# Constant rows of the key and query stacks: two memsets in place of one, and eight source rows in place of four

## The chip, the cores and the metric

The kernel runs on one core of one Trainium2 chip. The metric is the time of one execution on the device in microseconds (us), as the median of several runs; lower is better.

## The reference

Two branches read the same 2048 tokens of 512 features and are mixed by a gate of each token:

```
x = A_x                                           # 1 x 2048 x 512
g = sigmoid((x * gate_w).sum(-1, keepdims=True))
# a: attention, 32 heads of 16, each query sees itself and the 255 tokens before it
q, k, v = split(x @ wqkv);  scores = q.k * 16**-0.5, masked to the band
a = softmax(scores) @ v @ wo
# b: channel MLP, 512 -> 1792 -> 512
b = gelu(layernorm(x) @ w1 + b1) @ w2 + b2
out = g * a + (1 - g) * b
```

## The kernel before, in words

Every matmul operand is split into a high part and a low part, and products are summed from three matmuls (high by high, low by high, high by low). TensorE is thus the busiest engine.

The program has three stages. The first (to about 169 us) makes q, k and v from x, 512 tokens at a time, and at the same time the statistics of the layer norm and the normalised input of the MLP. The second runs the attention of eight groups of four heads and fills TensorE's gaps with the MLP's first product, in an order written out as a string. The third is the MLP's second product and the output product of the attention. The change touches the first stage alone.

**The stacks.** `qk` is one SBUF tensor of 128 partitions with four planes of 2048 columns: planes 0 and 1 (`qs`) hold queries, planes 2 and 3 (`ks`) keys. A head's 16 features stand in 48 rows (high, high or low, low), and two heads stand above each other with four rows between them, which carry a correction by the row maximum: on the keys' side those four rows are minus one, on the queries' side they start as zero. The data goes through DRAM: `qk_out` (L316) writes every 512 tokens of q and k into the tensor `qkd[g]` (the profile calls it `qk` too), one for each of four head groups `g`, whose slots are `HR` = 52 rows of 2048 numbers; `load_stacks` (L347; its DMA is L351) reads 100 rows by four planes back from it into partitions 14 to 113 of `qk`. The four rows between two heads (rows 48 to 51 of every second slot) are put into DRAM by `gaps(g)` (L219; its DMA is L222), once for each group: one DMA of zeros for the queries' slots (t = 0) and one of minus ones for the keys' slots (t = 1), 4 blocks of 4 rows of 8 KB each. The source of both is `qk` itself, before it is filled, in partitions that `load_stacks` never writes.

**Where the constants come from.** On GpSimd (POOL), `masks_first` (L200) zeroes partitions 0 to 31 of the keys' planes, and `masks` (L204) zeroes those of the queries' planes (L206), sets partitions 96 to 127 of all four planes to minus one (L207) and builds the small masks `tri` and `wide`. Behind that on POOL stand memsets of `v` (L584) and a part of the splitting of x (`lo_part`, L134).

**What sets the order.** A table of steps, one for each unit of 12 or 24 matmuls: `masks_first` stands at step 2, `masks` at step 3, `gaps(g)` at steps 8, 16, 20 and 24, the first four `load_stacks` at steps 11, 19, 29 and 44, and the first score blocks `s_pair` (matmul L364, which read `qk`) at steps 16, 18, 20 and so on. Each engine works through its own instructions in this order. Nearly all DMAs are issued by SyncE (SP), a few (`put(act, 0, h)` in `qk_out`) by ScalarE (ACT). The completion of these DMAs is counted on eight semaphores in turn (DMAHW0 to DMAHW7), and a DMA that takes one of them waits for the DMA that had it before. So a later DMA can be held up by an earlier one with which it shares no data.

Of the kernel before, what the change touches and what calls it, by code (L numbers as in the profile page):

```python
# [19 lines left out]
S = 2048  # L20
# [11 lines left out]
HG = H // NG  # L32
VW = 17
VR = 560
HR = 52
# [27 lines left out]
def gated_mix_kernel(ctx, tc: tile.TileContext, xt, x2, wq0, wqk, wv, wo, xa, gw, w1, w2, b1, b2, out):  # L63
    nc = tc.nc
    dve, act, pool, pe, sp = nc.vector, nc.scalar, nc.gpsimd, nc.tensor, nc.sync
# [18 lines left out]
    def get(key, tag, bufs, shape, dt=F32):  # L84
        return left[key].tile(list(shape), dt, name=nm(tag), tag=tag, bufs=bufs)
# [38 lines left out]
    def small(tag, bufs, shape, dt=F32):  # L124
        return consts.tile(list(shape), dt, name=nm(tag), tag=tag, bufs=bufs)

    def view(t, *ap, off=0):
        return bass.AP(tensor=t.tensor, offset=t.offset + off, ap=[list(x) for x in ap])

    def f32(t):  # L130
        return t.bitcast(F32)
# [31 lines left out]
    qkd = [dram.tile([2, HG, HR, S], F32R, name=f"qk{g}") for g in range(NG)]  # L163
# [3 lines left out]
    qk = get("ring", "qk", 1, (128, 4, S), F32R)  # L167
    qs, ks = [qk[:, pr] for pr in range(2)], [qk[:, 2 + pr] for pr in range(2)]
# [35 lines left out]
    def masks():  # L204
        for t in qs:
            pool.memset(f32(t[:32]), 0.0)  # L206
        pool.memset(f32(qk[96:128]), -1.0)  # L207
        one = small("scr", 2, (128, 256), BF16)
        pool.memset(one, 1.0)
        pool.affine_select(out=one[:, :128], in_=one[:, :128], pattern=[[-1, 128]], base=0, channel_multiplier=1,  # L210
                           compare_op=ALU.is_ge, fill=0.0)
        for e in range(2):
            pool.tensor_copy(tri[:, e], one[:, :128])
        pool.memset(wide, 0.0)
        pool.memset(rt, 0.0)
        pool.affine_select(out=wide[:, 128:], in_=wide[:, 128:], pattern=[[-1, 128]], base=0, channel_multiplier=1,
                           compare_op=ALU.is_ge, fill=NEG)

    def gaps(g):  # L219
        for t in range(2):  # L220
            dst = view(qkd[g], [S, 4], [2 * HR * S, 4], [1, S], off=(t * HG * HR + 48) * S)
            sp.dma_start(f32(dst), f32(qk[124 * t:124 * t + 4]))  # L222

    wq, wvs, xh, xl = {}, [], [], []

# [357 lines left out]
    for i in range(4):  # L583
        at((3, 5, 6, 8)[i], lambda i=i: pool.memset(vs[:, 4 * i:4 * i + 4], 1.0))  # L584
    at(2, masks_first)
    at(3, masks)
    at(9, load_consts)
    for g in range(NG):
        at((8, 16, 20, 24)[g], lambda g=g: gaps(g))
# [199 lines left out]
    t = spare[0]  # L789
# [183 lines left out]
```

## Time and profile before

| | |
|---|---|
| median of 3 runs | 720.65 us (718.29 to 720.96) |
| the profiled execution's own time | 715.11 us |
| its span | 713.1 us, granted TensorE clock 0.99 in the mean |
| TensorE matmul (PE) busy | 688.7 us, 97% of the span |
| VectorE (DVE) / ACT / POOL busy | 479.6 / 384.3 / 270.5 us |
| moved by DMA | 138.42 MB, mean 194 GB/s |

A row of a timeline has the start, the duration, engine, line, operation, what is written and read, how many instructions are merged in it (x12), and in brackets how long the engine sat idle before it and what ended that. SPq is SP's sequencer; its rows are issues of DMAs, and their duration is the time that the issue took, not the transfer. A row of the windows has the stretch, its length, the busy time and instructions of the five engines, the granted TensorE clock (1.00 is full speed), the mean busy share of the 16 DMA engines and the GB/s that they moved.

### The profile page before, as it was taken

What the parts mean: (1) busy time and instruction counts of PE and PEld (TensorE: products, weight loads), DVE (VectorE), ACT (ScalarE), POOL (GpSimd) and SP (SyncE); (2) the same over time, 40 slices, a digit from 0 to 9 for tenths busy, and PEclk for the clock granted to TensorE, in tenths of its full rate; (3) what the DMA queues carried; (4) which work ended last, traced back from release to release, by engine and by line L of the source; (5) the groups of instructions that cost most, each with busy time, mean ns of one, the idle gap of its engine ahead of it and who ended that gap; (6) DMA issues with size and microseconds to landing.
All of it is one profiled execution on the core that took longest, in us unless ns stands there. A gap on an engine that the chain in (4) does not pass through costs nothing.

```text
span 713.1 us, 15508 instructions
## 1 busy us (share of the span) xinstructions
PE 688.7 (97%) x5674; PEld 537.8 (75%) x5674; DVE 479.6 (67%) x970; ACT 384.3 (54%) x637; POOL 270.5 (38%) x621
## 2 busy tenths in 40 slices
PE   9996897999999999999999999999999999999997
PEld 6675675787776877777787777877788888888886
DVE  6825555997777778777867788784675645646554
ACT  6315344344767777687676776767753323224131
POOL 6900104652666666576555664747500000000000
PEclk9998999999999999999999999999999999999999
DMA  9868767878766676757766756644686541750801
GB/s 327 295 197 245 202 162 225 258 226 260 219 217 189 175 228 211 232 154 212 226 209 186 224 165 187 184 148 145 230 289 225 182 154 40 213 178 9 268 8 60
DMA packets 88987, 138.42 MB, mean 194 GB/s; under 512 B 12048, under 2 KB 35984, under 8 KB 88784
## 3 DMA queue, kind: packets, MB, share of 16 engines
q1 hardware_dynamic: 80752, 129.24, 58.2%
q10 hardware_dynamic: 8160, 8.19, 4.0%
q8 instruction: 45, 0.74, 0.4%
q14 instruction: 30, 0.25, 0.1%
HBM read 82.06 MB, written 54.30 MB: 191 GB/s over the span
## 4 chain that ended last, share of the span: by engine, by line
PE 76%; DMA 13%; DVE 6%; ACT 2%; SPq 1%; issue 1%; ACTq 0%; POOL 0%; DVEq 0%
PE ps_a L882 21%; PE ps_b L652 20%; PE ps_b L442 12%; PE ps_b L419 7%; PE ps_b L364 6%; PE ps_o L851 6%; DMA t<-in_xa 4%; DMA qk<-qk 3%; DMA t<-in_x 2%; PE ps_d L309 2%; PE ps_d L341 2%; DMA t<-in_wqk 2%; DVE x L134 1%; DVE t L533 1%; DVE wv L236 1%
## 5 line engine op out<-in xcount | busy, mean ns | idle before, releaser
L652 PE MATMUL ps_b<-x,w 64*128 64x512 f32 x1344 | 207.3, 393 | 0.0
L882 PE MATMUL ps_a<-x,t 128*128 128x512 f32 x648 | 149.6, 389 | 0.0
L374 DVE TENSOR_REDUCE mx<-ps_b 128x2 f32<-128x512 f32 x208 | 144.1, 693 | 7.1
L882 PEld LDWEIGHTS ps_a<-x,t 128*128 128x128 f32 x648 | 121.6, 188 | 25.3
L652 PEld LDWEIGHTS ps_b<-x,w 64*128 64x128 f32 x1344 | 127.1, 186 | 10.7 <-ACT x L137 0.3
L373 DVE COPY_PREDICATED ps_b<-tri,ps_b 128x256 f32<-128x256 uint8 x208 | 88.3, 425 | 54.7 <-PE ps_b L364 42.1
L423 POOL TENSOR_SCALAR_AFFINE_SELECT pa<-pa 128x256 f32<-128x256 f32 x192 | 74.2, 414 | 56.3 <-ACT pa L421 55.3
L309 PE MATMUL ps_d<-x,w 128*128 128x512 f32 x360 | 89.6, 406 | 3.1 <-ACT v L137 3.1
L421 ACT ACTIVATE pa<-ps_b 128x768 f32<-128x768 f32 x96 | 76.6, 813 | 25.2 <-PE ps_b L419 14.5
L419 PE MATMUL ps_b<-qk 50*128 50x384 f32 (+5 forms) x512 | 88.0, 340 | 0.1
L309 PEld LDWEIGHTS ps_d<-x,w 128*128 128x128 f32 x360 | 70.5, 197 | 19.5 <-ACT v L137 3.6
L364 PE MATMUL ps_b<-qk 62*128 62x384 f32 (+3 forms) x472 | 83.1, 346 | 1.7 <-DMA qk<-qk 1.3
L421 ACT ACTIVATE pb<-ps_b 128x768 f32<-128x768 f32 (+2 forms) x96 | 66.2, 707 | 20.1 <-PE ps_b L419 10.5
L423 POOL TENSOR_SCALAR_AFFINE_SELECT pb<-pb 128x256 f32<-128x256 f32 x160 | 62.3, 415 | 37.8 <-ACT pb L421 37.2
L708 ACT ACTIVATE t<-t,b1s 128x512 f32<-128x512 f32 x56 | 38.6, 716 | 44.3 <-DMA t<-hp 43.8
L419 PEld LDWEIGHTS ps_b<-qk 50*128 50x128 f32 (+1 forms) x512 | 48.7, 184 | 16.7 <-issue 3.2
L423 POOL TENSOR_SCALAR_AFFINE_SELECT x<-x 128x256 f32<-128x256 f32 x128 | 49.3, 414 | 30.4 <-ACT x L421 29.9
L364 PEld LDWEIGHTS ps_b<-qk 62*128 62x128 f32 (+1 forms) x472 | 45.0, 184 | 18.6 <-issue 3.7
L421 ACT ACTIVATE x<-ps_b 128x768 f32<-128x768 f32 x64 | 50.7, 813 | 15.0 <-PE ps_b L419 10.9
L341 PE MATMUL ps_d<-wv,x 128*128 128x512 f32 x192 | 48.5, 399 | 1.1 <-DVE wv L236 0.8
L851 PE MATMUL ps_o<-w,t 128*128 128x512 f32 x192 | 46.1, 389 | 0.0
L341 PEld LDWEIGHTS ps_d<-wv,x 128*128 128x128 f32 x192 | 35.4, 188 | 11.9 <-DVE wv L236 2.0
(96 smaller groups left out, 772.3 us busy)
## 6 DMA issues: line engine op xcount, KB each, us to landing
qk<-qk SPq DMA_DIRECT2D x56, 400.0 KB
t<-hp SPq DMA_DIRECT2D x56, 256.0 KB
hp<-t SPq DMA_DIRECT2D x54, 256.0 KB
qk<-t SPq DMA_DIRECT2D x48, 256.0 KB
osc<-x SPq DMA_DIRECT2D x31, 256.0 KB
t<-in_w SPq DMA_DIRECT2D x28, 256.0 KB
w<-w SPq DMA_DIRECT2D x28, 256.0 KB
qk<-t ACTq DMA_DIRECT2D x24, 256.0 KB
```

The source lines that it names most:

```text
L309: pe.matmul(o, a[:, dt * 128:(dt + 1) * 128], b[:, dt * C:(dt + 1) * C], start=n == 0, stop=n == 11)
L341: pe.matmul(o, x[:, a:a + 128], wvs[dt][:, k], start=n == 0, stop=n == 11)
L364: pe.matmul(o[:, e, :n], qs[pr][r:k, qb * 128:qb * 128 + 128], ks[pr][r:k, t0:t0 + n], start=True, stop=True)
L373: dve.copy_predicated(o[:, :, :128], tri, o[:, :, 256:384])
L374: dve.tensor_reduce(m, o[:, :, :256], mybir.AxisListType.X, ALU.max)
L419: pe.matmul(o[:, e, :w], ks[pr][r:k, kb * 128:kb * 128 + 128], qs[pr][r:k, kb * 128:kb * 128 + w], start=True, stop=True)
L421: act.activation(pt[:, :, :w], o[:, :, :w], AF.Exp, scale=0.25)
L423: pool.affine_select(out=pt[:, :, a:a + 128], in_=pt[:, :, a:a + 128], pattern=[[0, 2], [sgn, 128]], base=b, channel_multiplier=-sgn, comp ...
L442: pe.matmul(a[32 * h:32 * h + 32, at:at + w], vs[:, kb, v:v + 32], pts[p, kb][:, h, fr:fr + w], start=n == 0, stop=n == len(parts) - 1, sk ...
L652: pe.matmul(o[:, e], w[kt // 4][r:r + 64, k, m:m + 128], y[r:r + 64, a:a + C], start=n == 0, stop=n == 23)
L851: pe.matmul(a, x[:, g], wos[g][:, k], start=n == 0, stop=n == 11)
L882: pe.matmul(accs[c][b], x[:, b * 128:(b + 1) * 128], w, start=f == 0 and n == 0, stop=f == FT - 1 and n == 2)
```

## The change

The memset of minus ones is made for the keys' two planes, one instruction each, and no longer for the queries' planes. The planes of the queries thus have no minus ones to copy from, so `gaps` takes all its rows from the keys' planes: eight partitions with both planes (16 KB in one piece each) in place of four partitions with four planes. Zeros come from partitions 0 to 7 (before: 0 to 3), minus ones from partitions 116 to 123 (before: 124 to 127). In DRAM the same rows are written; each partition now fills two neighbouring rows of one block, where before a partition filled one row in each of the four blocks.

```diff
     def masks():
         for t in qs:
             pool.memset(f32(t[:32]), 0.0)
-        pool.memset(f32(qk[96:128]), -1.0)
+        for k in ks:
+            pool.memset(f32(k[96:128]), -1.0)
         one = small("scr", 2, (128, 256), BF16)
...
     def gaps(g):
         for t in range(2):
-            dst = view(qkd[g], [S, 4], [2 * HR * S, 4], [1, S], off=(t * HG * HR + 48) * S)
-            sp.dma_start(f32(dst), f32(qk[124 * t:124 * t + 4]))
+            dst = view(qkd[g], [2 * HR * S, 4], [2 * S, 2], [1, 2 * S], off=(t * HG * HR + 48) * S)
+            sp.dma_start(f32(dst), f32(qk[116 * t:116 * t + 8, 2:].rearrange("k r s -> k (r s)")))
```

On POOL the rows from the memsets of the stacks on are, before (a name carries a running number; L207 is the memset of minus ones, 8192 numbers in each of 32 partitions):

```order
L206 MEMSET qk_75 32x2048 x2
L207 MEMSET qk_75 32x8192
L209 MEMSET scr_268 128x256
L210 ISA
L210 AFFINE_SELECT scr_268<-scr_268 128x128
```

and after:

```order
L206 MEMSET qk_75 32x2048 x2
L208 MEMSET qk_75 32x2048 x2
L210 MEMSET scr_269 128x256
L211 ISA
L211 AFFINE_SELECT scr_269<-scr_269 128x128
```

The one memset of 8192 numbers a partition is now two of 2048; nothing else on POOL has moved.

On SP, at the first call of `gaps`, before (`qk_65` is the DRAM tensor of group 0, `qk_75` the SBUF stacks; behind the two L222 stand a load of weights and stores of q and k):

```order
L322 DMA qk_65<-t_343 16x8x512 [waits DMAHW2_49,DVE_49]
L222 DMA qk_65<-qk_75 4x4x2048 [waits DMAHW3_49,Pool_49]
L222 DMA qk_65<-qk_75 4x4x2048 [waits DMAHW4_49,Pool_49]
L229 DMA t_394<-in_wqk 128x512 [waits DMAHW5_49]
L322 DMA qk_65<-t_409 16x8x512 [waits DMAHW6_49,Activation_49]
L322 DMA qk_65<-t_409 16x8x512 [waits DMAHW7_49]
```

and after:

```order
L323 DMA qk_65<-t_344 16x8x512 [waits DMAHW2_49,DVE_49]
L223 DMA qk_65<-qk_75 4x2x4096 [waits DMAHW3_49,Pool_49]
L223 DMA qk_65<-qk_75 4x2x4096 [waits DMAHW4_49,Pool_49]
L230 DMA t_395<-in_wqk 128x512 [waits DMAHW5_49]
L323 DMA qk_65<-t_410 16x8x512 [waits DMAHW6_49,Activation_49]
L323 DMA qk_65<-t_410 16x8x512 [waits DMAHW7_49]
```

The order and the waits are the same; the shape that the two DMAs write goes from 4x4x2048 to 4x2x4096. At the other three calls it is the same, and PE, DVE and ACT have the same rows with the same waits as before (line numbers behind the memset are higher by one).

## The prediction

> **What bounds the kernel.** I read the page's first two parts, then TensorE's waits in the first 170 us, where the changed lines lie, then PE's and SP's timelines there, and last windows over the stretches in which little moves. First the page: busy time, and tenths in 40 slices of 17.8 us.
>
> ```profile
> PE 688.7 (97%) x5674; PEld 537.8 (75%) x5674; DVE 479.6 (67%) x970; ACT 384.3 (54%) x637; POOL 270.5 (38%) x621
> PE   9996897999999999999999999999999999999997
> ```
>
> TensorE is the bound nearly everywhere; only slices 4, 5 and 7 (53 to 89 and 107 to 125 us) have holes. A change in the first stage is worth what it takes out of them. Who ends them (engine, tile, line; us, times, longest):
>
> ```profile
> PE ps_x L364 <- DMA qk<-qk: 10.3, 2, 7.1
> PE ps_d L309 <- ACT v L137: 3.1, 1, 3.1
> PE ps_x L364 <- DVE mx L374: 2.2, 2, 1.6
> ```
>
> and where they lie on PE:
>
> ```profile
> 49.90 2.88 PE L309 MATMUL ps_d<-x,w 128*128 128x512 f32 x12
> 59.87 0.69 PE L364 MATMUL ps_x<-qk 62*128 62x128 f32 x4 [7.09 <-DMA qk<-qk]
> 60.48 4.44 PE L309 MATMUL ps_d<-x,w 128*128 128x512 f32 x12
> 89.44 0.62 PE L364 MATMUL ps_x<-qk 62*128 62x384 f32 x4 [3.22 <-DMA qk<-qk]
> 113.24 7.36 PE L309 MATMUL ps_d<-x,w 128*128 128x512 f32 x24 [3.14 <-ACT v L137]
> 122.15 0.44 PE L364 MATMUL ps_x<-qk 62*128 62x384 f32 x2 [1.55 <-DVE mx L374]
> ```
>
> The two largest end when `load_stacks` lands. The same twelve matmuls take 2.88 us before the first hole and 4.44 us right behind it, 1.56 us more. So the holes hold 7.09 + 3.22 + 3.14 + 2.2 = 15.65 us, and 3 x 1.56 = 4.7 us if the second and third cost as much in slow matmuls: 20.3 us in all. This is the ceiling of a gain here.
>
> Why does `load_stacks` land late? SP's own rows (start, time of the issue), at the first, second and fourth `gaps` (L222):
>
> ```profile
> 32.50 1.04 SPq L222 DMA_DIRECT2D qk<-qk  x2
> 33.60 4.33 SPq L229 DMA_DIRECT2D t<-in_wqk  x1
> 38.02 3.71 SPq L322 DMA_DIRECT2D qk<-t  x1
> 45.29 0.48 SPq L229 DMA_DIRECT2D t<-in_wqk  x1
> 48.76 0.31 SPq L351 DMA_DIRECT2D qk<-qk  x1
> 65.82 0.84 SPq L222 DMA_DIRECT2D qk<-qk  x2
> 71.39 4.74 SPq L469 DMA_DIRECT2D t<-in_xa  x1
> 79.22 0.31 SPq L351 DMA_DIRECT2D qk<-qk  x1
> 97.50 0.61 SPq L222 DMA_DIRECT2D qk<-qk  x2
> 103.69 3.78 SPq L398 DMA_DIRECT2D qk<-md  x1
> ```
>
> The issue of a weight load takes 0.48 us at 45.29 us and 4.33 us right behind `gaps`; behind three of the four calls SP is stuck for 3.7 to 4.7 us at a time. Windows in those stretches (the last two figures are the share of the 16 DMA engines and GB/s), with one of undisturbed loads ahead:
>
> ```profile
> 10.00:20.00 10.00, 10.00 (x46) 8.28 (x45) 10.00 (x13) 6.07 (x12) 9.48 (x4) 1.00 1.05 404
> 36.00:38.00 2.00, 2.00 (x11) 1.65 (x10) 0.69 (x1) 0.60 (x1) 0.47 (x1) 1.00 0.24 25
> 70.00:72.00 2.00, 2.00 (x10) 1.66 (x9) 1.65 (x11) 1.73 (x5) 0.00 (x0) 1.00 0.31 32
> 106.00:108.00 2.00, 2.00 (x11) 1.27 (x10) 0.00 (x0) 0.00 (x0) 0.00 (x0) 1.00 0.17 18
> ```
>
> At full load the 16 engines move 404 GB/s, 25 each. At 36 us, 0.24 x 16 = 4 engines are busy and move 25 GB/s together: four engines at the rate of one. A `gaps` DMA has four partitions as source and four outer rows as destination. I read this as four engines that each take one partition, through one path into SBUF that carries 25 GB/s. Every other transfer has a share on those four engines and queues behind. So the constant rows are the choke of this stage, and not the memset.
>
> **The change part by part.** Sizes of the DMAs:
>
> ```profile
> qk<-qk SPq DMA_DIRECT2D x8, 128.0 KB
> ```
>
> *The DMAs of `gaps`.* A call moves 2 x 128 KB = 262 KB (decimal); at 25 GB/s that is 10.5 us, of which the stretch from the issue at 32.50 us to the return of normal issues at about 44.8 us is made. After, the bytes, the number of DMAs and the four outer destination rows are the same, but each DMA reads eight partitions, two for each engine. The trace has no DMA of eight rows, so its rate is bounded: at least 25 GB/s (all eight rows on one path: no gain), at most 100 GB/s (four engines at 25 each: 2.6 us a call). I take 50 GB/s. 404 GB/s over 128 rows is 16 paths of 25 GB/s, 8 rows each on the average, and four neighbouring rows were seen to share one; so eight neighbours need not fit on one path, and two paths is the nearest case. Then a call takes 5.2 us, 5.2 us less.
>
> Here a rule bears on the case. The Trainium skill (SBUF — State Buffer, Door 1: The DMA port swizzle) says that four neighbouring partitions share a port, and partitions 32 higher come back to it. By it 0 to 3 and 4 to 7 are on two ports, as are 116 to 119 and 120 to 123; with its ~27 GB/s a port, a call would take an estimated 4.9 us, and the sum below would differ by 0.3 us a call. The row at 36 us agrees for four partitions; no run here shows eight yet. The same skill (DMA: Bandwidth & Descriptors, Why a DMA increments its semaphore by 16 and not by 1) has a DMA use the largest number of engines up to 16 that divides the outer dims of both sides: 4 with 4 before, 4 with 8 after, so it speaks against any relief by more engines. The share of 0.24 agrees with four.
>
> *First hole.* `load_stacks` is issued at 48.76 us behind the stuck issues and lands at 59.87. If all moves up by 5.2 us, 1.9 us of the 7.09 stay. Is the matmuls' slow stretch gone too? Windows (granted clock is the third figure from the right):
>
> ```profile
> 59.90:64.80 4.90, 4.90 (x17) 3.92 (x18) 3.04 (x7) 3.94 (x10) 0.00 (x0) 0.63 0.92 320
> 118.50:124.00 5.50, 3.33 (x16) 2.18 (x15) 5.36 (x13) 2.33 (x6) 3.11 (x10) 1.00 0.78 227
> ```
>
> Behind the 7.09 us hole the clock is 0.63; over the two short waits on DVE (2.2 us together) it stays 1.00. With 1.9 us left I count the 1.56 us as saved. Term: 5.2 + 1.56 = 6.8 us.
>
> *Second hole.* The second pair's issue at 65.82 us is tied to PE's progress (it stands behind stores of its results), so it moves with PE, and the pair is again 5.2 us shorter; `load_stacks` at 79.22 us stands behind it. 5.2 is over 3.22, so the hole closes, with its slow matmuls: 4.8 us.
>
> *Third hole.* PE waits for ACT, and ACT sat idle until just before, released by one of its own issues of a store:
>
> ```profile
> 111.13 0.63 ACT L472 ACTIVATE waste<-t 128x512 f32<-128x512 f32 x1 [9.07 <-DMA qk<-t]
> ```
>
> This is the fourth pair's stretch (97.50 to about 110 us). Closed in full it is worth 3.14 + 1.56 = 4.7 us. But ACT also waits for loads of `in_xa` that lie in the same queues, so I take half, 2.3 us. The short waits on DVE I leave at nothing: DVE is busy 5.36 of 5.5 us there (the window above).
>
> *The memset.* POOL and DVE:
>
> ```profile
> 12.38 3.56 POOL L206 MEMSET qk<- 32x2048 f32 x2
> 16.00 6.95 POOL L207 MEMSET qk<- 32x8192 f32 x1
> 25.32 1.97 POOL L584 MEMSET v<- 128x2240 f32 x1
> 28.41 4.24 POOL L134 TENSOR_TENSOR x<-v,x 128x512 fp32r<-128x512 f32 x3 [1.12 <-ACT x L137]
> 16.89 7.72 DVE L236 CAST wv<-t 128x512 fp32r<-128x512 f32 x4
> 45.15 0.43 DVE L195 CAST w<-t 128x512 fp32r<-128x512 f32 x1 [7.33 <-DMA t<-in_wqk]
> 23.29 7.73 PE L341 MATMUL ps_d<-wv,x 128*128 128x512 f32 x24 [0.76 <-DVE wv L236]
> ```
>
> Two memsets of 2048 take 3.56 us where one of 8192 takes 6.95: POOL gains 3.4 us. What stands behind is done 3.4 us earlier up to 28.41 us, where POOL waits for ACT anyway. `gaps` is first issued at 32.50 us, 9.5 us after the memset's end: no gain there. One thing could be: four casts on DVE take 1.93 us each while POOL writes, where the same cast takes 0.43 later, and PE waits on them. But POOL's next memset of `v` moves up to 21.9 us and covers the fourth cast again, and what PE saves before 52 us it waits longer in the first hole. I count 0; the bounds are 0 and 0.76 us. The cover is the first hole; if the DMAs shrink so far that it closes, up to 0.76 us comes back.
>
> **Sum.** 6.8 + 4.8 + 2.3 = 13.9 us. The profiled execution took 715.11 us (span 713.1) and would take 701.2; it lies 5.5 us below the median of the three runs, 720.65, on which it gives 706.8. I say 707.
>
> **The rivals.** *One path in part.* If the 16 paths are blocks of eight neighbours, partitions 0 to 7 lie on one path and only 116 to 123 straddle two: a call goes from 10.5 to 7.9 us. The 404 GB/s row allows it as well. Then the first hole loses 2.6 us and keeps its slow clock, the second closes to 0.6 us and loses 2.6 + 1.56, the third half of 2.6: 8.1 us in the best case, about 5 if the holes follow by half: 713 to 716.
>
> *The choke is not at the rows read.* Four engines writing into one DRAM tensor could share the limit on that side, or the transfer is late for another reason; then eight rows read at 25 GB/s as four did, and only POOL's 3.4 us go, off the path: 720 to 721. For it speaks that no row tells source from destination; against it, that stores of results to DRAM do not show such windows.
>
> *Slower.* The destination of an engine changes too: before, the four engines wrote four neighbouring rows of one block, now each writes its own block, 104 rows of 8 KB away from the next. If the limit is at the DRAM side and blocks at that distance collide, a call gets longer. The slowest row above has 18 GB/s; at that, a call takes 14.6 us, 4.1 more. Passed on through three holes it is +12 us: 733. It decides from the point where the rate with only these transfers under way falls below 25 GB/s. Nothing in the trace speaks for it beyond that row, which is the tail of a call with fewer engines at work (share 0.17).
>
> **How the numbers follow.** A difference under 0.5% (3.6 us) is about what a measurement of this kernel cannot tell from none. Two paths for each DMA, 10 to 18 us gained: 0.62. Half the effect, 4 to 10 us: 0.18. No change: 0.14. Slower: 0.06. So faster 0.80, same 0.14, slower 0.06. The range goes from 701 (all holes of 20.3 us closed) to 718 (below it 0.62 + 0.18 and a little of "no change"; slower left out); the likeliest case's own is 702 to 711.
>
> **What would show it.** In the profile of the changed kernel: the windows with only `gaps` under way show 50 GB/s at a share near 0.25 and are half as long; the issue behind `gaps(0)` takes 1 to 2 us in place of 4.33; PE's hole before the first L364 is 1 to 3 us and the twelve matmuls behind it take 2.88 us; the hole at 89 us is gone. POOL's two memsets take 3.56 us and PE's wait on the casts stays near 0.76. I am wrong if the GB/s in those windows stay at 25, or if they double and another transfer (`in_xa`, `in_x`) keeps PE's holes as long as they are.

## The result and the profile after

The changed kernel takes 698.75 us (median of 4 runs, 697.51 to 699.18), the kernel before 719.71 us beside it (4 runs, 718.29 to 720.96): ratio 0.9707, 95% interval 0.9681 to 0.9732. That is 21 us faster where 13.9 were predicted, and below the stated range. A later measurement on another chip gave 699.48 us, ratio 0.9727 (0.9708 to 0.9746), 19.6 us by the ratio. The profiled execution took 697.51 us with a span of 695.5 us, 17.6 us shorter than before's 713.1.

Busy time and the tenths of PE in 40 slices, of the page of the changed kernel:

```profile
PE 684.8 (98%) x5674; PEld 537.5 (77%) x5674; DVE 475.4 (68%) x970; ACT 384.6 (55%) x637; POOL 268.2 (39%) x622
PE   9989999999999999999999999999999999999997
```

The three dents of before are one shallow one. Who ended PE's waits in the first 170 us, in the changed kernel (line numbers are one higher than before):

```profile
PE ps_x L365 <- DMA qk<-qk: 2.7, 1, 2.7
PE ps_x L365 <- DVE mx L375: 1.0, 2, 0.6
```

The waits for `load_stacks` fell from 10.3 to 2.7 us, the wait for ACT is gone. On PE's timeline:

```profile
22.78 5.60 PE L342 MATMUL ps_d<-wv,x 128*128 128x512 f32 x24
47.26 2.88 PE L310 MATMUL ps_d<-x,w 128*128 128x512 f32 x12
52.83 0.69 PE L365 MATMUL ps_x<-qk 62*128 62x128 f32 x4 [2.69 <-DMA qk<-qk]
53.45 5.49 PE L310 MATMUL ps_d<-x,w 128*128 128x512 f32 x12
80.92 5.76 PE L310 MATMUL ps_d<-x,w 128*128 128x512 f32 x24
98.97 5.60 PE L310 MATMUL ps_d<-x,w 128*128 128x512 f32 x24
```

Two things here were not forecast. The 24 matmuls on `wv` (first row) take 5.60 us without a wait, where they took 7.73 behind a wait of 0.76: PE reaches the first hole 2.64 us earlier (50.14 for 52.78). And behind a hole of only 2.69 us the twelve matmuls take 5.49 us, more than the 4.44 of before (granted clock 0.50 from 53.40 to 58.70 us). The second hole and its slow matmuls are gone as forecast; the third, of which half was forecast, is gone whole. The 24 matmuls behind them take 5.76 and 5.60 us, before 7.35 (the row below) and 7.36:

```profile
89.98 7.35 PE L309 MATMUL ps_d<-x,w 128*128 128x512 f32 x24
```

SP's issues at the first call of `gaps` (now L223) in the changed kernel:

```profile
29.37 1.43 SPq L223 DMA_DIRECT2D qk<-qk  x2
30.86 1.26 SPq L230 DMA_DIRECT2D t<-in_wqk  x1
42.84 0.32 SPq L352 DMA_DIRECT2D qk<-qk  x1
```

The load behind it is issued in 1.26 us (before 4.33), and `load_stacks` at 42.84 us (before 48.76). But the call itself is also 3.1 us earlier, which the prediction had ruled out. (The predicted sign of 50 GB/s at a share near 0.25 cannot be read off the windows of the changed kernel, since other transfers are under way too: from 63.90 to 64.90 us the share is 0.50, with 104 GB/s. The packets further below show the rate.) The source of the earlier call is on VectorE; the casts of `wv` before and after (minimum, median, maximum of the four in ns):

```profile
L236 DVE CAST wv<-t x4: 500/554/6342, 16.9 to 24.1; 128x512 fp32r<-128x512 f32 x4
```

```profile
L237 DVE CAST wv<-t x4: 503/894/2111, 17.4 to 21.1; 128x512 fp32r<-128x512 f32 x4
```

The mean of 1.93 us that the prediction used was no mean of four alike: one cast was held for 6.34 us, to the end of the long memset (22.95 us), the other three took about half a microsecond.

### The profile page after: what moved, and what is told of

Read it like the earlier page. It is cut to its first block, busy times and chain, and to the rows that moved or that the text cites. A ratio compares the mean times of both kernels' runs of the same rounds, so it can differ in the third digit from the quotient of the medians.

```text
span 695.5 us, 15509 instructions
## 1 busy us (share of the span) xinstructions
PE 684.8 (98%) x5674; PEld 537.5 (77%) x5674; DVE 475.4 (68%) x970; ACT 384.6 (55%) x637; POOL 268.2 (39%) x622
## 4 chain that ended last, share of the span: by engine, by line
PE 87%; DMA 8%; DVE 2%; ACT 1%; issue 0%; SPq 0%; ACTq 0%; POOL 0%; DVEq 0%
PE ps_a L883 22%; PE ps_b L653 21%; PE ps_b L443 12%; PE ps_d L310 8%; PE ps_b L420 7%; PE ps_b L365 6%; PE ps_o L852 6%; PE ps_d L342 4%; DMA qk<-qk 3%; DMA t<-in_x 1%; DMA gws<-in_gw 1%; DMA wv<-in_wq 1%; DVE t L477 1%; DMA stat<-ms 0%; DVE mx L375 0%; ACT x L422 0%
## 5 line engine op out<-in xcount | busy, mean ns | idle before, releaser
L420 PE MATMUL ps_b<-qk 64*128 64x384 f32 (+5 forms) x512 | 88.6, 340 | 0.1
L310 PE MATMUL ps_d<-x,w 128*128 128x512 f32 x360 | 87.4, 399 | 0.0
L365 PE MATMUL ps_b<-qk 62*128 62x384 f32 (+2 forms) x472 | 83.5, 346 | 1.0 <-DMA qk<-qk 0.8
L310 PEld LDWEIGHTS ps_d<-x,w 128*128 128x128 f32 x360 | 68.8, 192 | 15.4 <-issue 0.5
L342 PE MATMUL ps_d<-wv,x 128*128 128x512 f32 x192 | 47.0, 395 | 0.0
L443 PE MATMUL ps_b<-pa,v 128*32 128x128 f32 (+2 forms) x704 | 42.9, 345 | 0.7 <-POOL pb L424 0.4
```

Of the source, the lines that this page charges most:

```text
L310: pe.matmul(o, a[:, dt * 128:(dt + 1) * 128], b[:, dt * C:(dt + 1) * C], start=n == 0, stop=n == 11)
L342: pe.matmul(o, x[:, a:a + 128], wvs[dt][:, k], start=n == 0, stop=n == 11)
L365: pe.matmul(o[:, e, :n], qs[pr][r:k, qb * 128:qb * 128 + 128], ks[pr][r:k, t0:t0 + n], start=True, stop=True)
L420: pe.matmul(o[:, e, :w], ks[pr][r:k, kb * 128:kb * 128 + 128], qs[pr][r:k, kb * 128:kb * 128 + w], start=True, stop=True)
L443: pe.matmul(a[32 * h:32 * h + 32, at:at + w], vs[:, kb, v:v + 32], pts[p, kb][:, h, fr:fr + w], start=n == 0, stop=n == len(parts) - 1, sk ...
```

## The experiments

Each kernel was measured beside runs of the kernel before on the same chip, in three sets of runs on three chips. Before's medians in them were 718.20, 718.38 and 718.63 us; ratios are to these, and gains in us are worked out from the ratios unless medians are named.

**The memset alone.** Four neighbouring source partitions, in the changed kernel's order of the destination.

```diff
-        pool.memset(f32(qk[96:128]), -1.0)
+        for k in ks:
+            pool.memset(f32(k[96:128]), -1.0)
...
-            dst = view(qkd[g], [S, 4], [2 * HR * S, 4], [1, S], off=(t * HG * HR + 48) * S)
-            sp.dma_start(f32(dst), f32(qk[124 * t:124 * t + 4]))
+            dst = view(qkd[g], [2 * HR * S, 4], [2 * S, 2], [1, 2 * S], off=(t * HG * HR + 48) * S)
+            src = f32(qk[124 * t:124 * t + 4, 2:].rearrange("k r s -> k (r s)"))
+            sp.dma_start(f32(dst), src.unsqueeze(1).broadcast_to([4, 2, 2 * S]))
```

> The memset's part alone, with the destination order of the changed kernel: minus ones only in the keys' planes, and each of the four engines writes its own block in pieces of 16 KB, but the source is four neighbouring partitions (0 to 3, 124 to 127), each read twice. Theory A (four neighbouring partitions share one path of 25 GB/s; the memset's worth is a separate 2.6 us, since VectorE's first cast is blocked for as long as the memset runs, 6.34 us before): 2 to 4 us faster than before, 716 to 718; the window with only these transfers under way stays at about 25 GB/s with a share of 0.25, and PE's first hole stays near 7 us but begins 2.6 us earlier. Rival B (the memset is hidden by the first hole, as predicted): within 1 us of before. Rival C (the limit is on the DRAM side, and the new order of the blocks or the pieces of 16 KB relieve it): 18 us or more faster, the window at 50 GB/s.

Measured: 716.31 us, ratio 0.9971 (0.9953 to 0.9989). A window of this kernel with almost only these transfers under way, and PE's first hole:

```profile
33.00:34.50 1.50, 1.50 (x9) 1.23 (x8) 0.32 (x1) 0.60 (x1) 0.00 (x0) 1.00 0.33 33
```

```profile
57.56 0.69 PE L366 MATMUL ps_x<-qk 62*128 62x128 f32 x4 [7.73 <-DMA qk<-qk]
```

0.33 x 16 = 5.3 busy engines move 33 GB/s, 6.3 each, as before (25 by 3.8 engines, 6.5 each). So neither the new order in DRAM nor pieces of 16 KB relieve the choke, and rival C falls. The kernel gains 2.1 us (0.8 to 3.4). The hole stays but begins 2.95 us earlier, at 49.83 us (57.56 less 7.73), and does not grow by as much (7.73 us for 7.09), because `gaps` is issued earlier too (its row stands in the next section). So B falls as well, though the interval of the time alone would not quite exclude it. This run has the new order of the destination as well; no run has the shorter memset with the old order.

**The eight rows alone.** `gaps` as in the change, the memset as before.

> The eight source rows alone; the memset still covers all four planes (6.95 us). Theory A: 17 to 18.5 us faster than before, 701 to 703, thus 2 to 4 us slower than the changed kernel; the first cast on VectorE takes 6.3 us again, the window shows 50 GB/s. Rival B (memset hidden): 698 to 699, as the changed kernel.

Measured: 702.10 us, ratio 0.9784 (0.9758 to 0.9810), 15.5 us by the ratio. The rows carry most of the gain. Its casts are held for 5.74 us again.

**Four rows, moved by two partitions.**

```diff
-            sp.dma_start(f32(dst), f32(qk[124 * t:124 * t + 4]))
+            sp.dma_start(f32(dst), f32(qk[2 + 120 * t:6 + 120 * t]))
```

> The kernel before with the four source partitions moved by two: 2 to 5 for zeros, 122 to 125 for minus ones; memset, shape and destination as before. Theory A (paths are groups of four partitions starting at multiples of four): two partitions on each of two paths, so the transfers take half as long, and the kernel is 16 to 18.5 us faster than before, 701 to 704. Rival D (a path is a block of eight neighbours, or what counts is the number of source rows): no change, 719 to 721, window at 25 GB/s. Rival C (DRAM side): no change.

Measured: 703.49 us, ratio 0.9802 (0.9772 to 0.9831). Nothing but the partitions' numbers differs from before, and 14.2 us go. A window in the first call:

```profile
35.50:36.50 1.00, 1.00 (x6) 0.84 (x5) 0.35 (x1) 0.00 (x0) 1.00 (x1) 1.00 0.29 66
```

0.29 x 16 = 4.6 engines move 66 GB/s, 14 each, twice the rate of before. It is not the number of rows but the border that the range straddles: 2 to 5 and 122 to 125 lie on two paths each, 0 to 3 and 124 to 127 on one each. The prediction's rival of blocks of eight neighbours falls with it (2 to 5 are in one such block). The port map of the Trainium skill (SBUF — State Buffer, Door 1: The DMA port swizzle) has its border there; here the runs agree.

**Four rows, four partitions apart.** The changed kernel with another source:

```diff
-            sp.dma_start(f32(dst), f32(qk[116 * t:116 * t + 8, 2:].rearrange("k r s -> k (r s)")))
+            src = f32(qk[115 * t:115 * t + 13:4, 2:].rearrange("k r s -> k (r s)"))
+            sp.dma_start(f32(dst), src.unsqueeze(1).broadcast_to([4, 2, 2 * S]))
```

> The changed kernel with four source partitions four apart (0, 4, 8, 12 and 115, 119, 123, 127), each read twice, so that by theory A each of the four engines has a path to itself: a call of gaps takes 2.6 us (100 GB/s at a share of 0.25), the first hole of 2.7 us and the slow matmuls behind it (5.49 us for twelve in place of 2.88) go, 3 to 5.5 us faster than the changed kernel, 693 to 696. Rival E (with 50 GB/s the constant rows no longer bound anything, the loads behind them do): within 1.5 us of the changed kernel, 697 to 700.

Measured: 695.13 us, ratio 0.9680 (0.9657 to 0.9704), 3.6 to 4.4 us under the changed kernel's two medians. A window in the second call, and the place of the first hole on PE:

```profile
56.50:57.50 1.00, 1.00 (x6) 0.82 (x5) 0.91 (x3) 0.77 (x3) 0.00 (x0) 1.00 0.35 131
```

```profile
46.86 2.88 PE L311 MATMUL ps_d<-x,w 128*128 128x512 f32 x12
49.67 0.44 PE L366 MATMUL ps_x<-qk 62*128 62x128 f32 x4
50.04 2.99 PE L311 MATMUL ps_d<-x,w 128*128 128x512 f32 x12
```

5.6 engines move 131 GB/s, 23 each, near the 25 of undisturbed loads. The first hole is closed, and the twelve matmuls behind it run at full speed. 6.5, 14 and 23 GB/s for an engine with four, two and one of them on a path: the rate is divided among those that share it.

These windows hold some other traffic too, and their rates are estimates. The traces settle it, for they hold every DMA packet with its start, duration and size, and the packets of `gaps` differ by their size from those beside them on the queue: 8 KB, or 16 KB where both planes go out in one piece, against 2 KB. The first call, from its first packet to the end of its last:

| kernel | source partitions | first call |
|---|---|---|
| before | 0 to 3, 124 to 127 | 34.72 to 44.16 us, 9.4 us |
| memset alone | the same | 31.78 to 41.63 us, 9.9 us |
| eight rows alone | 0 to 7, 116 to 123 | 34.90 to 41.18 us, 6.3 us |
| changed kernel | the same | 31.33 to 37.17 us, 5.8 us |
| moved by two | 2 to 5, 122 to 125 | 34.98 to 40.82 us, 5.8 us |
| four apart | 0, 4, 8, 12 and 115, 119, 123, 127 | 30.46 to 33.80 us, 3.3 us |

In before the commonest time of an 8 KB packet is 1.25 us (9 of 32, 6.5 GB/s), and the shortest 0.31 us. With the rows moved by two 13 of 32 take 0.31 us and the next commonest time is 0.63 us (4). With spread rows 15 of 16 packets of 16 KB take 0.61 us (26.8 GB/s). So a packet takes about four, two or one times the shortest, as four, two or one engines share a path.

**One call at a time.** Memset as before; eight rows in the first call only, in the second only, in the third and fourth only.

```diff
+            if g == 0:    # or g == 1, or g > 1: the changed source and destination
+                ...
+            else:         # those of before
```

> The memset as before; only the first call of gaps takes its rows from eight partitions, the other three from four. The prediction's term for the first hole: 6.8 us faster than before. From the profile of the eight rows alone (first hole 3.03 us in place of 7.09, the twelve matmuls behind it still slow): 4 to 5 us faster, 713 to 714.5.

> As the run on the first call, but only the second call takes eight rows. The prediction's term for the second hole: 4.8 us faster than before, 713.4. If the first call's delay is what makes the second hole: under 2 us faster.

> As the run on the first call, but only the third and the fourth call take eight rows. The prediction's term for the third hole, counted at half: 2.3 us faster than before, 716. If the wait on ScalarE ends with the fourth call's transfers alone, the hole closes whole, with its slow matmuls and the waits on VectorE behind it: 4.5 to 6.5 us faster, 712 to 714.

Measured: first call 714.31 us, ratio 0.9942 (0.9917 to 0.9966), 4.2 us; second 714.64 us, 0.9941 (0.9919 to 0.9962), 4.2 us; third and fourth 712.15 us, 0.9907 (0.9874 to 0.9940), 6.7 us. The sum of 15.1 us is that of the eight rows alone (15.5): the calls add up. The holes do not divide as cleanly: with only the last two calls changed the third hole is gone and the wait for ACT with it, but the second shrinks too, from 3.22 to 1.59 us without slow matmuls, and a wait of 2.35 us on VectorE follows at 118.20 us. With only the first call changed, PE shows

```profile
54.73 0.44 PE L368 MATMUL ps_x<-qk 62*128 62x128 f32 x4 [1.82 <-DMA qk<-qk]
55.10 4.60 PE L313 MATMUL ps_d<-x,w 128*128 128x512 f32 x12
110.03 7.35 PE L313 MATMUL ps_d<-x,w 128*128 128x512 f32 x24 [4.15 <-ACT v L137]
```

A hole of 1.82 us, nearly the 1.9 that the prediction left, still costs slow matmuls; and the third hole stands as long as the last calls are slow.

**The memset in pieces.** Eight rows, and the memset over all four planes in 16 instructions of 512.

```diff
-        pool.memset(f32(qk[96:128]), -1.0)
+        for n in range(16):
+            pool.memset(f32(qk[96:128, n // 4, n % 4 * C:n % 4 * C + C]), -1.0)
```

> Eight rows as in the changed kernel; the memset of all four planes is as large as before (8192 numbers a partition) but cut into 16 instructions of 512. If a cast on VectorE is kept out for the whole of the POOL instruction that runs (one block of 6.3 us behind one long memset): the four casts take 2 to 4.5 us together though POOL writes as long as before, and the kernel gains 1.5 to 3 us on the run with eight rows alone, 699 to 701. If POOL's writing slows the casts in proportion (1.9 us each, as the mean of the row suggests): the casts take 7 us and the time stays at 701 to 703.

Measured: 703.07 us, ratio 0.9772 (0.9735 to 0.9808), not told from the eight rows alone. POOL and the casts:

```profile
16.05 7.47 POOL L208 MEMSET qk<- 32x512 f32 x16
```

```profile
L237 DVE CAST wv<-t x4: 500/554/6845, 17.0 to 24.7; 128x512 fp32r<-128x512 f32 x4
```

Both theories missed. The casts are not slowed in proportion (three take half a microsecond), but the first is not let in between 16 instructions back to back either: it waits 6.85 us, to the end of the last (23.52 us). In this run what counts is when POOL's run of writes ends.

**The memset shorter.** Spread rows; minus ones in one plane only.

```diff
-        for k in ks:
-            pool.memset(f32(k[96:128]), -1.0)
+        pool.memset(f32(ks[0][96:128]), -1.0)
...
+            dst = view(qkd[g], [2 * HR * S, 4], [S, 4], [1, S], off=(t * HG * HR + 48) * S)
+            src = f32(ks[0][115 * t:115 * t + 13:4])
+            sp.dma_start(f32(dst), src.unsqueeze(1).broadcast_to([4, 4, S]))
```

> The spread rows (0, 4, 8, 12 and 115, 119, 123, 127), with minus ones in one plane of the keys alone, which each of the four source partitions reads four times: POOL's memset takes 1.8 us in place of 3.6. If the length of POOL's writing still counts once the constant rows are quick: the casts take 2.5 us in place of 4.2 and the kernel gains another 1 to 2 us on the run with spread rows, 693 to 694. If PE has no hole left in which it could show: 694 to 696.

Measured: 693.07 us, ratio 0.9653 (0.9630 to 0.9677), the fastest kernel of this study, some 6 us under the changed one. Its casts:

```profile
L237 DVE CAST wv<-t x4: 503/556/1206, 16.9 to 19.0; 128x512 fp32r<-128x512 f32 x4
```

The four take 2.59 us, as the first theory had it. But that the 2.1 us to the spread rows come from this is not shown. They are from two sets of runs, and the intervals of the ratios overlap. And in the profiles PE is no earlier: its first twelve matmuls behind the first `s_pair` begin at 50.19 us, with spread rows at 50.04. The two part at 100 us, where the kernel with spread rows waits on VectorE for 1.36 and 0.61 us and its next twelve matmuls take 4.61 us, this one for 0.58 and 0.62 us and 3.02.

**The changed kernel again, and with the full memset in four instructions** (`for k in ks + qs`).

> The changed kernel itself, beside the others of this call on the same chip: 697.5 to 700; it says how much the next kernel's larger memset costs, and the spread rows gain, without a change of chip.

> The changed kernel with the memset of minus ones over all four planes again, but as four instructions of 2048 in place of one of 8192: only POOL's 3.5 us of extra writing tell it from the changed kernel. If the memset is worth what its run alone gained (2 us): 1.5 to 3 us slower than the changed kernel in this call. If with quick rows it is worth more (SP reaches the first call of gaps later by the whole delay of the casts): 3 to 5 us slower. If hidden: under 1 us.

Measured: 699.48 us (0.9727, 0.9708 to 0.9746) and 700.95 us (0.9755, 0.9734 to 0.9777): 1.5 us between the medians, and the intervals overlap. The three kernels with eight rows and the full memset, in one instruction, in sixteen and in four, gain 15.5, 16.4 and 17.6 us by their ratios; the changed kernel gains 21.1 and 19.6. So with quick rows the shorter memset is worth 2.0 to 5.6 us, and against the memset in one instruction the intervals do not overlap (0.9758 to 0.9810, and 0.9746 at most).

Why it varies shows in the two profiles. With the full memset the first cast is held for 6.44 us again, and the 24 matmuls ahead of PE's last longer wait in this stage begin at 100.71 us, 2.8 us later than the changed kernel's 97.93. Then the changed kernel loses most of it at that wait, on VectorE:

```profile
106.00 0.69 PE L365 MATMUL ps_x<-qk 62*128 62x384 f32 x2 [2.48 <-DVE mx L375]
107.68 5.15 PE L342 MATMUL ps_d<-wv,x 128*128 128x512 f32 x12
```

The other waits 1.13 and 0.62 us there and has its twelve matmuls at 3.03 us. In its first profile the changed kernel waited only 0.35 and 0.62 us at this place. What makes this wait long in one execution and short in the next stays open.

## Why the prediction was wrong

Right were the reading of what bounds the stage (the constant rows, not the memset's own time), the choke (four engines on one path), the choice of two paths (5.2 us a call, 5.8 by the packets of the first), and the direction. Wrong was the size, since three of its terms and its ceiling were off. The rows alone come to 702.10 us, inside the stated range; what takes the change below it is the memset, which the prediction put at nothing. And that the rows' three terms add up to 13.9 us, near the 15.5 measured, is luck: the first is too large and the third too small.

| term | predicted | measured |
|---|---|---|
| first hole (first call) | 6.8 us | 4.2 us |
| second hole (second call) | 4.8 us | 4.2 us |
| third hole (calls three and four) | 2.3 us | 6.7 us, with part of the second |
| memset | 0 us | 2.1 us alone, 2.0 to 5.6 beside the rows |
| sum | 13.9 us | 17.2 us with the memset alone; whole change 19.6 to 21.1 by the two ratios |

*The third hole* is the largest miss among the rows. I took half, since ACT also waits for loads of `in_xa`. But these loads lie in the queues behind the same transfers, and with only the last two calls changed the hole is gone whole. In the changed kernel ACT still waits, for 5.91 us in place of 9.07:

```profile
93.98 0.63 ACT L473 ACTIVATE waste<-t 128x512 f32<-128x512 f32 x1 [5.91 <-DMA t<-in_xa]
```

and PE no longer notices. So the discount for another wait in the same queue counted the same cause against itself. The waits on VectorE behind it, left at nothing, fell from 2.2 to 1.0 us in this profile but were 3.0 us in the second one of the same kernel.

*The memset.* The step "`gaps` is first issued at 32.50 us, 9.5 us after the memset's end: no gain there" looked only at the semaphore between the two. The path runs over a third engine: the memset holds the first cast, the cast holds VectorE's next low part of q or k in its queue, SP's store of that low part waits for it, and `gaps` stands behind the store on SP. In before the low part ends at 25.21 us, the store goes out right behind it, and the weight load and the other stores ahead of `gaps` follow:

```profile
24.53 0.68 DVE L134 TENSOR_TENSOR t<-ps_d,t 128x512 fp32r<-128x512 f32 x1
25.23 0.52 SPq L322 DMA_DIRECT2D qk<-t  x1
25.80 1.12 SPq L229 DMA_DIRECT2D t<-in_wqk  x1
```

With the memset alone that low part begins at 21.05 us, and `gaps` is issued 3 us earlier:

```profile
29.53 1.04 SPq L224 DMA_DIRECT2D qk<-qk  x2
```

And "what PE saves before 52 us it waits longer in the first hole" failed for the same reason, since the transfers move up too. The error began with the mean of the group of casts: "1.93 us each while POOL writes" was one blocked instruction.

*The first hole.* The call was to shrink by 5.2 us; by its packets it shrank by 3.6 (9.4 to 5.8). The hole was to shrink to 1.9 us; it is 1.82 us with the first call alone, and 2.69 and 2.89 us in the two profiles of the changed kernel. But the term failed above all on the clock: from two short waits without a lowered clock I concluded that 1.9 us would be harmless, and counted 1.56 us as saved. Behind 1.82 us the twelve matmuls took 4.60 us, behind 2.69 us 5.49. What decides can be read from the granted clock. In every trace of this study it changes only on a grid of 3.41 us. Cut along this grid, the kernel with only the first call changed shows a stretch with the whole hole in it (PE busy 1.60 of 3.42 us), and behind it half the clock for one stretch; in the kernel with the memset in pieces, waits of 1.94 and 0.62 us on VectorE fall across two stretches, and the clock stays:

```profile
52.66:56.08 3.42, 1.60 (x10) 1.15 (x9) 0.00 (x0) 0.72 (x2) 0.00 (x0) 1.00 0.99 327
56.08:59.49 3.41, 3.41 (x9) 2.65 (x9) 2.87 (x7) 3.21 (x8) 0.00 (x0) 0.50 1.03 359
```

```profile
104.90:108.32 3.42, 1.85 (x9) 1.19 (x7) 3.32 (x9) 2.45 (x6) 1.52 (x4) 1.00 0.75 223
108.32:111.73 3.41, 2.43 (x11) 1.79 (x12) 3.38 (x7) 0.90 (x2) 2.67 (x10) 1.00 0.81 217
```

Between 20 and 168 us of the thirteen traces, all 25 stretches at full clock in which PE is idle for 1.81 us or more are followed by half the clock, and none in which it is idle for 1.59 us or less. The two waits of before that misled me (1.55 and 0.62 us) fell across two stretches, with 0.99 and 1.18 us idle. The Trainium skill (TensorE: Matmul & The Clock Gate, Part 1) describes a free-running window of 3.4 us by which the clock is set, and a lowered clock after an idle one. The grid agrees; that a window must be wholly idle does not, since 1.81 us of 3.41 were enough here.

*The ceiling* of 20.3 us counted idle time and slow matmuls behind holes, but not the 24 matmuls on `wv` that took 7.73 us for 5.60: PE counted as busy while its weight loads waited for the casts. With their 0.76 and 2.13 us it would have been 23.2 us, and the low end of the range some 3 us lower, under the measured time.

The parts measured alone add up to 17.2 us, the change to 19.6 at least. The intervals of the four parts, 1.3 to 2.4 us each way, cover the difference; whether the memset and the rows help each other is open. The profiled executions differ by only 17.6 us: the first hole of the kernel with slow rows is not the same in each (7.09 us in before's profile, 7.73 with the memset alone, 8.68 with only the last calls changed), and before's profiled execution lies 4.6 us under its median.

## What to carry to other kernels

Look at the partitions that a small DMA reads, not only at its bytes: here four neighbours starting at a multiple of four gave about 25 GB/s together, the same four rows two partitions further about twice that, and four apart about four times, and the issue of the weight load behind them fell from 4.33 to 1.26 us when eight rows took their place. Follow a late instruction through the queues of all engines before costing an edit at nothing; a semaphore that is long since set does not show that its producer is off the path. Look at minimum and maximum of a group before using its mean. And before counting a short hole as harmless, lay it on the grid on which the clock changes.

## What the runs showed of the hardware

- Partitions share DMA paths in groups of four from a multiple of four, in the ranges tried: by windows 6.3 to 6.5 GB/s for each engine with four engines on one group, 14 with two, 23 with one; by packets 8 KB in 1.25 us (before) and 16 KB in 0.61 us (spread rows).
- A cast on VectorE stays out through 16 POOL memsets back to back (6.85 us) and through four (6.44 us) as through one of 6.95 us (6.34 us). Between two memsets of 2048 one cast was let in in the changed kernel (1.18 us, the next 2.11), none with the spread rows, where the same two memsets held the first cast for 2.93 us.
- A hole on PE of 1.82 us was followed by matmuls at 4.60 us for twelve (full speed 2.88); two waits of 1.55 and 0.62 us on VectorE in before were not. In the stretches of the 3.41 us grid, 1.81 us of idle PE or more was always followed by half the clock, 1.59 us or less never.
